# Transposing normalised rows on VectorE from a quadrant-wise load, one scratch each for Q and K, and an earlier load of the output weights

## The chip, the cores and the metric

The kernel runs on one NeuronCore of a Trainium2 chip. The metric is the time of one execution on the device, in microseconds (us). The engines are named as the profile names them: PE is TensorE (matrix products), PEld its weight loads, DVE is VectorE, ACT is ScalarE, POOL is GpSimd, and SP is the engine that issues nearly all DMAs.

## The reference

One row of 2048 tokens of width 640 goes through two branches in parallel, whose results are added to the input:

```python
x = A_x
xn = _layernorm(x, axis=-1)                    # (x - mean) / sqrt(var + 1e-5)
return x + _A_ref(xn, A_wqkv, A_wo) + _B_ref(xn, B_w_gate, B_w_up, B_w_down)
```

The first branch is attention with 32 heads of 20 features in a causal window of 256 tokens. The second is a gated MLP of inner width 1536:

```python
# A: q, k, v = heads of xn @ wqkv;  p = softmax(q k^T / sqrt(20), window 256);  (p v) @ wo
# B: (sigmoid(xn @ w_gate) * (xn @ w_up)) @ w_down
```

Inputs and output are bf16.

## The kernel before

The tokens are cut into four chunks of 512. For a chunk, `xnT[c]` holds the normalised rows with features on the partitions (five groups of 128 features) and tokens along the free dimension. All projections read it: Q and K (`proj_block`, tile `pqk`, L319), V (`project_v`, tile `pv`, L349), gate and up (`g_gu`, tiles `pg` and `pu`, L436 and L443). A product's result lies in one of four PSUM banks with the tag `d`, and the bank comes free when VectorE or ScalarE has read it.

How `xnT` is made differs by chunk. For chunk 0, rows are normalised as they arrive and turned by TensorE (`transpose_rows`, L299). For chunks 1 to 3 the generator `g_norms` does it in small steps: `load_x` brings the chunk with one DMA (token on the partition, L159), VectorE takes two `bn_stats` and one `bn_aggr` for each block of 128 rows (L272, L278), GpSimd makes the four reciprocal roots with an addition and a power (`rstd_blocks`, L286 and L287), VectorE normalises each block (`norm_block`, L292), and `turn_block` turns it with a DMA transpose on SP's queue (L303). The tile `xc` that `load_x` fills has one buffer, so the next chunk's load waits for the last norm of this one.

A block of Q or K is evicted into a tile `st` (six buffers; VectorE for Q, L323, ScalarE for K, L325) and stored in a DRAM scratch (`sq`, `sk`, L327), from which `spread` (L337) reads it back with heads on the partitions. There are two scratches for each of Q and K, used by chunks in turn. Rows 20 to 31 of each head's group of 32 are set to zero once by `clear` (L198): for the first pair of scratches at the start, for the second by `clear_next`, later.

The output weights are rearranged through DRAM: `turn_wo` (L232) writes them to the scratch `wo_i` with eight DMAs, `load_wo` (L237) reads them into SBUF with four. `load_wd` (L225) brings the down weights with five.

Attention goes by steps of scores. In a step TensorE fills `ps` (L512), ScalarE takes the exponential into `pT` (L517), GpSimd masks diagonal and old edges (L524), and in some steps VectorE masks a shared piece (L529). A pair of head groups is finished by `pv` (tile `acc`, L543), whose result VectorE transposes, scales and transposes again (L555 to L571).

The order is written out by hand. The class `Fill` holds a list of labelled generators (gate and up, Q and K, V, output of a chunk), each yielding the cost of what it has just recorded, and the loop over steps pulls as much filling between two steps as an allowance says. `mix(a, b, first, every)` interleaves a generator `b` (here `g_norms`) with the steps of `a`: from step `first` on, one step of `b` after each `every` steps of `a`. Each engine runs its own instructions in the recorded order, and so does SP's queue: a DMA that waits holds back all that is recorded behind it.

## Time and profile before

| | |
|---|---|
| runs | 310.28, 312.11, 312.65 us; median 312.11 |
| profiled execution, its own time | 312.31 us |
| its span (first to last instruction) | 310.5 us |
| TensorE busy | 302.4 us (97% of the span) |
| TensorE clock granted | 1.0 throughout |
| VectorE, ScalarE, GpSimd busy | 172.0, 198.4, 165.3 us |
| DMA | 35.67 MB, mean 115 GB/s |

The span is what the trace covers, and the time of the execution is 1.8 us longer. Busy time is a sum over the whole span. What limits a stage is seen in the idle time of TensorE there and in what ended it. In a line of groups the columns are: kernel line, engine, operation, output and inputs, shapes, count, then busy time, mean time of one in ns, and idle time of the engine before them with what ended it.

### The profile page before, as it was taken

The numbers are of one execution on the slowest core, as the hardware profiler recorded it, in microseconds if no ns is written. First come the engines' busy times: TensorE is split into PE (matmuls) and PEld (weight loads), VectorE is DVE, ScalarE is ACT, GpSimd is POOL, SyncE is SP. The second block draws the span as 40 slices with busy tenths as digits, with TensorE's granted clock in tenths as the row PEclk, the third lists the DMA queues.
The fourth block names the chain that finished last, engine by engine and source line by source line (L and its number), as shares of the span: only waits on it lengthen the run. The fifth ranks groups of instructions, "written<-read, shape, count | busy, mean of one in ns | idle before, by whom it ended". The sixth has DMA issues, their size and how long they took to land.

```text
span 310.5 us, 10034 instructions
## 1 busy us (share of the span) xinstructions
PE 302.4 (97%) x4343; PEld 168.1 (54%) x4343; DVE 172.0 (55%) x342; ACT 198.4 (64%) x196; POOL 165.3 (53%) x304
## 2 busy tenths in 40 slices
PE   6999999998999999999989999999999999999996
PEld 3654444544657654554556665454546665444774
DVE  5633684828697464496945346373643626372533
ACT  6923868668964648888654548978675647778000
POOL 3020668457885828566661836747383756657000
PEclk9999999999999999999999999999999999999999
DMA  7997984985705453440013512640000210000201
GB/s 206 365 327 237 330 155 150 344 260 165 231 0 89 108 158 121 155 160 2 3 23 88 87 56 89 211 155 1 4 0 4 67 40 23 2 2 2 87 23 63
DMA packets 40459, 35.67 MB, mean 115 GB/s; under 512 B 10560, under 2 KB 39872, under 8 KB 40384
## 3 DMA queue, kind: packets, MB, share of 16 engines
q1 hardware_dynamic: 39552, 34.27, 37.2%
q10 hardware_dynamic: 864, 0.77, 0.9%
q8 instruction: 34, 0.56, 0.8%
q14 instruction: 9, 0.07, 0.1%
HBM read 23.63 MB, written 10.26 MB: 109 GB/s over the span
## 4 chain that ended last, share of the span: by engine, by line
PE 90%; DVE 4%; DMA 2%; ACT 2%; issue 1%; SPq 0%; DVEq 0%; ACTq 0%
PE y L457 17%; PE pu L443 17%; PE pg L436 16%; PE pqk L319 12%; PE ps L512 8%; PE pv L349 7%; PE y L464 7%; PE acc L543 6%; DMA sq<-st 1%; ACT pT L517 1%; DVE on L567 1%; DMA xc<-in_A_x_dram 1%; DVE st L323 1%; DVE xn L292 1%; DVE h L447 0%
## 5 line engine op out<-in xcount | busy, mean ns | idle before, releaser
L524 POOL TENSOR_SCALAR_AFFINE_SELECT pT<-pT 64x512 bf16<-64x512 bf16 (+1 forms) x252 | 153.6, 609 | 103.6 <-ACT pT L517 91.8
L517 ACT ACTIVATE pT<-ps 128x2048 bf16<-128x2048 f32 x75 | 140.8, 1877 | 60.4 <-PE ps L512 57.5
L447 DVE SCALAR_TENSOR_TENSOR h<-th,pu 128x512 bf16<-128x512 f32 x48 | 32.8, 683 | 54.3 <-PE pu L443 41.7
L443 PE MATMUL pu<-xnT,wu 128*128 128x512 bf16 x240 | 59.8, 380 | 0.0
L436 PE MATMUL pg<-xnT,wg 128*128 128x512 bf16 x240 | 59.8, 380 | 0.0
L457 PE MATMUL y<-wd,h 128*128 128x320 bf16 (+2 forms) x396 | 56.8, 295 | 0.8 <-DVE h L447 0.8
L319 PE MATMUL pqk<-xnT,wqkv 128*128 128x512 bf16 x200 | 46.0, 381 | 0.0
L457 PEld LDWEIGHTS <-h 128*128 128x128 bf16 x396 | 36.6, 98 | 17.0 <-issue 2.2
L439 ACT ACTIVATE th<-pg 128x512 f32<-128x512 f32 x48 | 28.6, 596 | 15.3 <-PE pg L436 15.1
L436 PEld LDWEIGHTS <-wg 128*128 128x128 bf16 x240 | 22.3, 98 | 25.6 <-issue 2.0
L443 PEld LDWEIGHTS <-wu 128*128 128x128 bf16 x240 | 22.1, 98 | 25.4 <-issue 1.8
L319 PEld LDWEIGHTS <-wqkv 128*128 128x128 bf16 x200 | 22.6, 119 | 18.8 <-issue 1.4
L512 PE MATMUL ps<-qT,kT 20*64 20x320 bf16 (+4 forms) x1456 | 32.2, 259 | 0.3 <-issue 0.2
L512 PEld LDWEIGHTS <-kT 20*64 20x64 bf16 x1456 | 15.9, 103 | 24.8 <-issue 21.8
L555 DVE STREAM_TRANSPOSE t<-acc 128x512 f32<-128x512 f32 x32 | 21.1, 696 | 13.3 <-PE acc L543 13.3
L567 DVE TENSOR_TENSOR on<-t,rec 128x320 bf16<-128x320 f32 (+4 forms) x48 | 27.7, 576 | 1.1
L468 DVE SCALAR_TENSOR_TENSOR rows<-y,rows 128x320 bf16<-128x320 f32 x30 | 14.4, 488 | 23.8 <-PE y L464 23.5
L349 PE MATMUL pv<-wqkv,xnT 128*128 128x320 bf16 x160 | 25.9, 300 | 0.0
L464 PE MATMUL y<-wo,oc 128*128 128x320 bf16 (+2 forms) x165 | 24.2, 295 | 0.0
L543 PE MATMUL acc<-pT,v 64*32 64x320 bf16 (+4 forms) x1456 | 19.8, 252 | 1.4 <-DVE pT L529 1.4
L358 DVE CAST v<-pv 64x320 bf16<-64x320 f32 x29 | 14.1, 487 | 12.2 <-PE pv L349 11.9
L543 PEld LDWEIGHTS <-v 64*32 64x32 bf16 x1456 | 16.3, 91 | 7.4 <-issue 2.6
(48 smaller groups left out, 157.3 us busy)
## 6 DMA issues: line engine op xcount, KB each, us to landing
qT<-sq SPq DMA_DIRECT2D x16, 256.0 KB
kT<-sk SPq DMA_DIRECT2D x16, 256.0 KB
sq<-st SPq DMA_DIRECT2D x20, 128.0 KB
sk<-st SPq DMA_DIRECT2D x20, 128.0 KB
out_dram<-rows SPq DMA_DIRECT2D x15, 160.0 KB
wg<-in_B_w_gate_dram SPq DMA_DIRECT2D x4, 480.0 KB
wu<-in_B_w_up_dram SPq DMA_DIRECT2D x4, 480.0 KB
xc<-in_A_x_dram SPq DMA_DIRECT2D x3, 640.0 KB
```

The costliest lines, as they stand in the source:

```text
L319: nc.tensor.matmul(ps, lhsT=wt[:, m, :], rhs=xnT[c][:, d, :], start=(d == 0), stop=(d == DC - 1))
L349: nc.tensor.matmul(ps[:, 0:HALF], lhsT=xnT[c][:, d, s * P:(s + 1) * P], rhs=wqkv[:, d, 2 * D + hf * HALF:2 * D + (hf + 1) * HALF], start=( ...
L436: nc.tensor.matmul(pg, lhsT=part(wg, d, f), rhs=xnT[c][:, d, :], start=(d == 0), stop=(d == DC - 1))
L443: nc.tensor.matmul(pu, lhsT=part(wu, d, f), rhs=xnT[c][:, d, :], start=(d == 0), stop=(d == DC - 1))
L447: nc.vector.scalar_tensor_tensor(out=h, in0=th, scalar=1.0, in1=pu, op0=ADD, op1=MULT)
L457: nc.tensor.matmul(y[:, 0:cut[1] - cut[0]], lhsT=ht[c, f][:, s * P:(s + 1) * P], rhs=wd[:, f, cut[0]:cut[1]], start=(f == 0), stop=False)
L464: nc.tensor.matmul(y[:, 0:cut[1] - cut[0]], lhsT=oc[c, m][:, s * P:(s + 1) * P], rhs=wo[:, m, cut[0]:cut[1]], start=False, stop=(m == DC - 1))
L512: nc.tensor.matmul(ps[a * U:(a + 1) * U, i, col * U:(col + n) * U], lhsT=qk["k", kc, o // GH][32 * i:32 * i + DH, o % GH + a, kb * U:(kb + ...
L517: nc.scalar.activation(out=pt[:, :, 0:CW], in_=ps, func=EXP, scale=SCALE)
L524: nc.gpsimd.affine_select(out=view, in_=view, pattern=[[0, HG], [0, n], [sign, U]], compare_op=GE, fill=0.0, base=base, channel_multiplier ...
L543: nc.tensor.matmul(acc[32 * i:32 * i + 32, q * U:(q + n) * U], lhsT=vt[kb][a * U:(a + 1) * U, u, h * VW:h * VW + 32], rhs=pt[a * U:(a + 1) ...
L567: nc.vector.tensor_tensor(out=on[m][:, :, slot:slot + n], in0=t1[:, :, first:first + n], in1=rec.to_broadcast([P, 16, n]), op=MULT)
```

## The change

- `load_x` brings a chunk with four DMAs. The quadrant of partitions 32q to 32q + 31 gets features 160q to 160q + 159, and token 32j + t of the chunk lies on partition t of each quadrant, slot j.
- With features spread over the quadrants, VectorE's transpose of 32 x 32 blocks gives `xnT` directly. `turn_block` uses it in place of the DMA transpose.
- Feature 5p + b is now on partition p of group b, so all weights that multiply `xnT` are loaded in that order (`by_feature`), and chunk 0's transposes read rows with a stride of five.
- Statistics of a row are in four quadrants. `moments` takes them with eight `bn_stats` a chunk (two rows interleaved in each), two small operations turn them into mean and mean square, and `sum_quarters` adds the quadrants with one f32 product on TensorE against a matrix of quarters, made once by sixteen small GpSimd instructions. `rstd_rows` makes the roots of 16 columns with four GpSimd instructions.
- `norm_rows` normalises 128 x 160 elements at a time, sixteen for a chunk. It reads with a stride of five and writes runs of 32.
- Q and K have one scratch each. `clear_next` is gone.
- `turn_wo` is recorded right after `load_rest`. `load_wo` is recorded between the down weights and the Q and K of chunk 1, ahead of that chunk's Q stores; before, it was recorded inside `g_qk(1)` behind four of them.
- The steps of `g_norms` are spaced anew, and in `out1` the norms of chunk 3 go with every step of the output instead of every third.

The core of the diff:

```diff
 def load_x(c):
-        nc.sync.dma_start(out=t, in_=xr[:, c * SBC:(c + 1) * SBC, :])
+        for q in range(4):
+            nc.sync.dma_start(out=t[32 * q:32 * q + 32].rearrange("p s (j e) -> p (s j) e", e=QF),
+                              in_=x2[c * CW:(c + 1) * CW, q * QF:(q + 1) * QF].rearrange("(j t) e -> t j e", t=32))
...
+    def by_feature(w):
+        return w.rearrange("(p b) n -> p b n", b=DC)
...
-    scratch = {(w, k): tc.dram_tile([H * 32, CW], BF16, name=f"s{w}{k}")
-               for w in "qk" for k in range(2)}
+    scratch = {w: tc.dram_tile([H * 32, CW], BF16, name=f"s{w}") for w in "qk"}
...
+    def make_quarters():
+        for q in range(4):
+            rows = slice(32 * q, 32 * q + 32)
+            for k in range(4):
+                nc.gpsimd.tensor_scalar(out=quarters[rows, 32 * k:32 * k + 32], in0=ident[rows, rows],
+                                        scalar1=0.25, scalar2=None, op0=MULT)
...
+    def moments(c, u, stats):
+        nc.vector.bn_stats(out=stats[:, u, :],
+                           in_=xc[c].rearrange("p s (j e) -> p (s j) e", e=QF)[:, 2 * u:2 * u + 2, :]
+                           .rearrange("p j e -> p e j"))
+    def sum_quarters(stats):
+        ps = ps_d.tile([P, CW], FP32, name="pm", tag="d")
+        nc.tensor.matmul(ps[:, 0:2 * NJ], lhsT=quarters,
+                         rhs=stats.rearrange("p u (k z) -> p (u k) z", k=2)[:, :, 1:3], start=True, stop=True)
+        mom = lnp.tile([P, NJ, 2], FP32, name="mom", bufs=1)
+        nc.vector.tensor_copy(out=mom.rearrange("p j z -> p (j z)"), in_=ps[:, 0:2 * NJ])
+        return mom
+    def rstd_rows(mom):
+        r = lnp.tile([P, NJ], FP32, name="rstds", bufs=1)
+        nc.gpsimd.tensor_tensor(out=r, in0=mom[:, :, 0], in1=mom[:, :, 0], op=MULT)
+        nc.gpsimd.tensor_tensor(out=r, in0=mom[:, :, 1], in1=r, op=SUB)
+        nc.gpsimd.tensor_scalar(out=r, in0=r, scalar1=EPS, scalar2=None, op0=ADD)
+        nc.gpsimd.tensor_tensor(out=r, in0=r, in1=neghalf, op=POW)
+        return r
+    def norm_rows(c, s, j, mom, rstd):
+        if j == 0:
+            xns[c, s] = lnp.tile([P, D], BF16, name="xn")
+        k = s * SBC + j
+        nc.vector.tensor_scalar(out=xns[c, s].rearrange("p (b j f) -> p j b f", j=SBC, f=32)[:, j],
+                                in0=xc[c][:, s, j * QF:(j + 1) * QF].rearrange("p (f b) -> p b f", b=DC),
+                                scalar1=mom[:, k, 0:1], scalar2=rstd[:, k:k + 1], op0=SUB, op1=MULT)
...
 def turn_block(c, s):
-        nc.sync.dma_start(out=xnT[c][:, :, s * P:(s + 1) * P], in_=xns.pop((c, s)), transpose=True)
+        nc.vector.transpose(out=xnT[c][:, :, s * P:(s + 1) * P],
+                            in_=xns.pop((c, s)).rearrange("p (b t) -> p b t", b=DC))
...
 def g_norms(c, turn, behind=0):
-        mvs = lnp.tile([P, SBC, nc.vector.BN_AGGR_DIM], FP32, name="mvs", bufs=1)
-        for s in range(SBC):
-            ln_block(c, s, mvs[:, s, :])
-            if s < SBC - 1:
-                yield 0
-        for _ in range(behind):
+        stats = lnp.tile([P, NJ // 2, nc.vector.BN_STATS_DIM], FP32, name="moments", bufs=1)
+        for u in range(0, NJ // 2, 2):
+            moments(c, u, stats)
+            moments(c, u + 1, stats)
             yield 0
-        rstds = rstd_blocks(mvs)
+        mean, dev = (stats.rearrange("p u (k z) -> p u k z", k=2)[:, :, :, z] for z in (1, 2))
+        sq = lnp.tile([P, NJ // 2, 2], FP32, name="sq", bufs=1)
+        nc.vector.tensor_tensor(out=sq, in0=mean, in1=mean, op=MULT)
+        nc.vector.scalar_tensor_tensor(out=dev, in0=dev, scalar=1.0 / QF, in1=sq, op0=MULT, op1=ADD)
+        for _ in range(2 + behind):
+            yield 0
+        mom = sum_quarters(stats)
+        rstd = rstd_rows(mom)
         for _ in range(4):
             yield 0
         for s in range(SBC):
-            norm_block(c, s, mvs[:, s, :], rstds[:, s:s + 1])
-            yield 0
+            for j in range(SBC):
+                norm_rows(c, s, j, mom, rstd)
+                if j == 1:
+                    yield 0
             if turn:
                 turn_block(c, s)
+            yield 0
...
 def g_qk(c):
-                if c == 1 and w == "q" and m == 3:
-                    load_wo()
...
     load_rest()
+    turn_wo()
...
-    norms3 = g_norms(3, False)
+    norms3 = g_norms(3, False, 2)
...
     fill.add("x2", later(load_x, 2), 0)
-    fill.add("wo_i", later(turn_wo), 0)
     fill.add("wd", later(load_wd), 0)
-    fill.add("pads", later(clear_next), 0)
+    fill.add("wo", later(load_wo), 0)
     fill.add("qk1", g_qk(1), 50 * MM)
...
-    fill.add("out1", mix(g_out(1, g_gu(2, 0, 1)), itertools.chain(norms3, g_turns(3)), 1, 3), OUT + GU)
+    fill.add("out1", mix(g_out(1, g_gu(2, 0, 1)), itertools.chain(norms3, g_turns(3)), 1, 1), OUT + GU)
```

## The prediction

> **What bounds the kernel now.** I read the page first (sections 1 and 4), then busy time in stretches of 3 us, then the waits, then groups by line with shapes kept apart, then the timeline of VectorE and GpSimd where the change works.
>
> ```profile
> PE 302.4 (97%) x4343; PEld 168.1 (54%) x4343; DVE 172.0 (55%) x342; ACT 198.4 (64%) x196; POOL 165.3 (53%) x304
> ...
> PE 90%; DVE 4%; DMA 2%; ACT 2%; issue 1%; SPq 0%; DVEq 0%; ACTq 0%
> ```
>
> TensorE is busy 302.4 of 310.5 us, and the chain that ended last is 90% TensorE. The idle 8.1 us is all that can be won. The stretches tell where it lies (first number after the stretch's length: TensorE busy):
>
> ```profile
> 69.00:72.00 3.00, 1.56 (x84) 0.91 (x68) 1.38 (x3) 2.27 (x4) 1.75 (x4) 1.00 0.54 158
> 156.00:159.00 3.00, 2.16 (x17) 1.37 (x15) 2.34 (x5) 1.10 (x1) 2.33 (x5) 1.00 0.30 60
> 306.00:309.00 3.00, 1.42 (x23) 1.25 (x20) 1.06 (x3) 0.00 (x0) 0.00 (x0) 1.00 0.36 109
> ```
>
> 2.4 us lie in the first 9 us and 3.1 us after 306, which the change leaves alone; 1.44 us at 69 and 0.84 us at 156 are the stalls it touches, with about 0.3 us in crumbs. So the most it can win is some 2.6 us, 0.8%. The waits name both stalls:
>
> ```profile
> ACT st L325 <- DMA sq<-st: 2.0, 1, 2.0
> ...
> PE acc L543 <- DVE pT L529: 1.4, 1, 1.4
> ...
> PE y L457 <- DVE h L447: 0.8, 1, 0.8
> ```
>
> At 69: ScalarE could not evict a K block because the buffer still belonged to a Q store that had not landed; the exp behind it was late, then VectorE's mask, then TensorE. At 156: the last h of chunk 1 stood on VectorE behind two norms of chunk 3 (1.59 us on the chain).
>
> **The change, part by part.** The prices:
>
> ```profile
> L571 DVE STREAM_TRANSPOSE oc<-on 128x512 bf16<-128x512 bf16 x20 | 14.2, 711 | 0.7
> ...
> L292 DVE TENSOR_SCALAR xn<-xc,mvs,rstds 128x640 bf16<-128x640 bf16 x12 | 7.4, 640 | 0.9 <-POOL rstds L287 0.9
> ...
> L287 POOL TENSOR_TENSOR rstds<-rstds,neghalf 128x4 f32<-128x4 f32 x3 | 3.2, 1061 | 0.3
> ...
> L292 DVE TENSOR_SCALAR xn<-xc,mv,rstd 128x640 bf16<-128x640 bf16 x2 | 0.9, 446 | 0.1
> ...
> L286 POOL TENSOR_SCALAR rstds<-mvs 128x4 f32<-128x4 f32 x3 | 0.7, 227 | 3.1 <-DVE mvs L278 2.9
> ```
>
> *Transposes.* Twelve DMA transposes (1.2 us of SP's queue each) go; they never held TensorE. VectorE gets four per chunk of 128x640. The bf16 128x512 one takes 711 ns, and the next instruction starts 0.64 us after it; 128 columns more at the 1.04 ns a column that its neighbours show (f32 sums: 490 ns for 320 columns, 291 for 128) make 0.77 us. So 3.1 us a chunk.
>
> *Norms.* Four of 128x640 become sixteen of 128x160 with a stride of five elements in. The trace has no strided one. Above: a norm of VectorE alone that does not speed up costs 157 ns + 160 x 1.04 = 0.32 us, 0.28 from start to start; contended it could be 0.5, since the 128x640 norms range from 405 to 930 ns while GpSimd works. Below: a quarter of 446 ns, with overlap, 0.14. I take n = 0.28, the row of single columns being nearest. 16n = 4.5 us a chunk against about 2.4 now.
>
> *Statistics.* Still eight bn_stats of 320 columns (472 ns); four aggregates (209 ns) give way to two small sums and a copy: equal.
>
> *GpSimd.* Two instructions on 4 columns become four on 16: three plain ones (227 ns each with little per column: 0.8 us) and the power. The power on 4 columns takes 1.06 us. If its cost over a plain one (0.83 us) is per instruction, 16 columns take 1.06; if per column, 0.23 + 4 x 0.83 = 3.6. A plain instruction on as many columns takes 0.23, so the extra is more likely per column; I take p = 2.5, nearer to that end.
>
> *A: chunk 1.* Here hidden work comes out on the path. In the built order the reciprocal roots now stand behind the masks of the third step of scores. Those ran here:
>
> ```profile
> 39.64 4.89 POOL L524 TENSOR_SCALAR_AFFINE_SELECT pT<-pT 64x512 bf16<-64x512 bf16 x8 [0.17 <-ACT pT L517]
> ...
> 42.57 1.11 DVE L292 TENSOR_SCALAR xn<-xc,mvs,rstds 128x640 bf16<-128x640 bf16 x2
> 44.02 0.69 DVE L447 SCALAR_TENSOR_TENSOR h<-th,pu 128x512 bf16<-128x512 f32 x1 [0.34 <-issue]
> 44.62 1.31 DVE L555 STREAM_TRANSPOSE t<-acc 128x512 f32<-128x512 f32 x2
> ```
>
> Half of these eight masks (39.64 to 42.1) are ahead of the roots, so the roots are ready at 42.1 + 0.8 + p = 45.4. Behind them on GpSimd are the fourth step's masks, for which TensorE's acc at 43.4 waits (it already shows a 0.4 us weight-load wait on them), and on VectorE everything behind the first norm: h, and the transposes that free acc's banks. From that norm to the last transpose VectorE has 16n + 4 x 0.77 + four h at 0.61 + 1.24 (acc) + two reciprocals 0.5 + three scalings 1.15 + one oc 0.64 = 9.0 + 16n us, back to back. TensorE wants the whole xnT at 54.96 (first pqk of chunk 1). Late by 42.9 + p + 9.0 + 16n - 55.0 = p + 16n - 3.1 = +3.9 us. The acc stall lies inside this. Ends: p = 1.06, n = 0.14 gives +0.2; p = 3.6, n = 0.5 gives +8.5.
>
> *B: chunk 2.* VectorE is full from 83.8 to 94 and does its norms behind the second block's rows and the scaling of a head pair; without norms that work ends at 101.7. Then come 16n, 3.1 and 0.9 (rows): 105.7 + 16n against pqk at 109.34, so 16n - 3.6 = +0.9 us (0 to +4.4).
>
> *C: chunk 3.* The norms now stand behind the last h of chunk 1: the 0.84 us stall goes. Twelve norms then lie among the rows of the first two blocks and delay a y bank by about 0.4: net -0.4 (-0.8 to +0.6). The transposes end near 176, five us ahead of pqk.
>
> *D: SP's queue at the Q stores.* The weight turn (8 issues, 5.0 us) moves to 36 to 42, where transposes were. But x for chunk 2 (now four issues) waits for the last norm of chunk 1, 9 us later than now relative to pqk, and wd (five issues), wo (four) and the ten Q and K stores of chunk 1 stand behind it. Counted from the first pqk: x at -0.8, wd 1.0 to 3.4, wo to 6.0, first Q store at 6.2 (now 5.06). Ahead of its data lie x, wd and wo, 3.4 MB, at the 330 GB/s of that stretch 10.4 us; the two clears, 0.79 MB, are gone. It lands about 0.4 us earlier than now, and the stall shrinks to 1.0: -0.4 (-1.4 to +0.6). One scratch adds no wait: the spreads that read it were done some 20 us before.
>
> *E: the head.* x for chunk 1 goes from 512 packets of 1280 B to 2048 of 320 B, ahead of Q and K stores. Packets under 512 B (one transpose alone, 156 to 159) and 1280 B ones (17 to 20) moved at:
>
> ```profile
> GB/s 0 0 0 0 0 0 0 0 0 0 0 0 0 0 0 0 0 0 0 58 174 225 225 218 212 225 205 225 201 151 55 10 0 0 218 0 0 0 0 0
> ...
> GB/s 358 348 358 399 348 379 399 348 358 393 382 355 577 369 331 355 389 341 335 345 280 246 246 161 123 140 123 106 140 96 215 113 147 119 150 218 253 287 335 317
> ```
>
> 655 KB at 215 instead of 370 GB/s is 1.3 us more. The queues are 45 to 54% idle at 25 to 27, which takes most of it; the first scores at 30.8 wait on that chain (0.4 us): +0.3 (0 to 1.3). The Trainium skill, "DMA: Bandwidth & Descriptors", Specifications, puts line rate at 512 B and up, with a read-modify-write below. By that rule the load would cost twice its time, 3.5 instead of 1.8 us; the trace's 215 against 370 agrees in kind, and the sum would be about 0.4 higher.
>
> *F: small.* Chunk 0's transposes load weights with a stride of five: such loads take 119 ns (wqkv) against 98 (xn): 20 x 21 ns, half of it covered, +0.2 (0 to 0.4). Three f32 matmuls of 32 columns: two inside stalls already counted, one +0.3 (0.1 to 0.9). Sixteen GpSimd instructions for the quarter matrix lie in its idle 18 to 33 us.
>
> Sum: 3.9 + 0.9 - 0.4 - 0.4 + 0.3 + 0.2 + 0.3 = +4.8 us on the profiled 312.31: **317.1**. The median of the runs is 312.11, so the same by either.
>
> **Rivals.** *VectorE keeps up* (not slower): a norm costs 0.14 and the power 1.06. Then A = 0.2, B = 0, C = -0.8, D = -0.4, E to F +0.6: 311.9. It decides once p + 16n falls below about 4. For it: 0.45 us for 640 columns shows a norm runs faster than a column per 1.04 ns. Against it: that row is unstrided. In the Trainium skill, "VectorE: DVE Perf Modes", What auto-detection actually checks, packing two 16-bit elements needs step 1, while using both ports needs only matching outer dimensions. By it the norm would keep half its speed-up, n about 0.2, which puts the sum at 314.9, in between.
>
> *GpSimd and VectorE hold each other up*: n = 0.5, p = 3.6. A = 8.5, B = 4.4: 325.2. For it: 446 ns in the head, where GpSimd rests, against 640 mean and 930 at most later. The Trainium skill, "SBUF — State Buffer", Who interferes with whom, says two-port VectorE operations and GpSimd shut each other out; those rows agree. Against it: sixteen short ones need not each meet a mask.
>
> *Small packets at half rate again*: E +1.3, and D turns to +0.6 as x for chunk 2 lands late: 319.4.
>
> **How the numbers follow.** Forecast 0.50, VectorE keeps up 0.30, mutual blocking 0.12, packets 0.08. About 1%, 3.1 us, is what a measurement of this kernel can tell from no change. Faster by that (under 309.0) is beyond all that can be won as counted: 0.05 for what I do not see. Same: nearly all of the first rival and a small part of the forecast, 0.33. Slower: 0.62. The range 310.0 to 323.0 takes in the first and third rival and cuts the second; the forecast's own is 314.5 to 320.5.
>
> **What would show it.** A: idle TensorE, or pqk waiting on VectorE's transpose, at 55 to 60, and the power near 2.5 us. B: the same near 110. C: no wait of y on h at 156. D: the eviction's wait on the Q store at 1 to 2 us. n and p can be read directly. The forecast is wrong if chunk 1's first pqk starts before 56.

## The result, and the profile after

The changed kernel takes **329.92 us** (median of 4 runs, 329.39 to 330.76) against 312.06 us for the kernel before on the same chip (310.28 to 312.65): ratio 1.0585, interval 1.0537 to 1.0633. It is 17.9 us slower, where +4.8 was forecast and +10.9 was the end of the range. The profiled execution took 329.81 us, span 328.1.

Busy time, the clock row and the shares of the chain, from the page of the changed kernel:

```profile
PE 307.8 (94%) x4349; PEld 170.0 (52%) x4349; DVE 195.7 (60%) x387; ACT 198.3 (60%) x196; POOL 176.3 (54%) x326
...
PEclk9999999699999997999999999999999999999999
...
PE 70%; DVE 10%; DMA 7%; POOL 5%; issue 3%; SPq 2%; ACT 2%; DVEq 0%; ACTq 0%; POOLq 0%
```

TensorE's share of the chain fell from 90 to 70%. Two things grew: its idle time, from 8.1 to 20.3 us, and its busy time, from 302.4 to 307.8 us though its work is the same but for three small matmuls. The clock row says why most of the second: in slices 8 and 16 the granted clock drops. (Of the busy time, the groups pqk and acc gained 4.0 us and the three new products took 1.0.) Stretches of 3 us around both places (busy time of PE, PEld, DVE, ACT, POOL, then granted clock, DMA share, GB/s):

```profile
60.00:63.00 3.00, 0.00 (x0) 0.00 (x0) 2.97 (x7) 1.07 (x1) 0.92 (x2) 0.54 0.00 0
63.00:66.00 3.00, 2.86 (x37) 1.11 (x45) 1.48 (x4) 0.00 (x0) 0.00 (x0) 0.50 1.05 203
...
120.00:123.00 3.00, 0.12 (x1) 0.00 (x0) 2.96 (x7) 0.00 (x0) 2.10 (x4) 1.00 0.15 55
123.00:126.00 3.00, 1.20 (x4) 0.53 (x4) 2.49 (x7) 0.00 (x0) 0.00 (x0) 0.85 0.00 0
126.00:129.00 3.00, 3.00 (x25) 0.88 (x22) 0.69 (x1) 1.48 (x1) 0.00 (x0) 0.59 0.83 200
```

At 60 and at 120 TensorE stands still while VectorE is full (2.97 and 2.96 of 3). These are the two starts of pqk that steps A and B of the prediction are about. When TensorE resumes, its clock is 0.50 for some 4 us, so the first matmuls take up to 631 ns instead of 379. The waits:

```profile
PE pqk L360 <- DVE xnT L343: 7.9, 2, 4.7
DVE xn L325 <- POOL rstds L318: 7.8, 2, 4.6
...
ACT st L366 <- DMA sq<-st: 3.5, 2, 2.5
...
PE acc L590 <- POOL pT L571: 2.2, 2, 2.0
```

The third line is the stall on the Q stores, which was to shrink. Groups by line, and the spread of the norm (minimum, median, maximum in ns):

```profile
L325 DVE TENSOR_SCALAR xn<-xc,mom,rstds 128x160 bf16<-128x160 bf16 x48 | 22.1, 511 | 7.8 <-POOL rstds L318 7.8
...
L318 POOL TENSOR_TENSOR rstds<-rstds,neghalf 128x16 f32<-128x16 f32 x3 | 8.8, 2939 | 0.2
```
```profile
L325 DVE TENSOR_SCALAR xn<-xc,mom,rstds x48: 341/448/817, 46.5 to 187.9; 128x160 bf16<-128x160 bf16 x48
```

The power takes 2.94 us (2.5 was taken). The norm runs from 341 to 817 ns. Chunk 2's sixteen on VectorE's timeline, in fours, with a GpSimd line beside the third four:

```profile
113.23 2.51 DVE L325 TENSOR_SCALAR xn<-xc,mom,rstds 128x160 bf16<-128x160 bf16 x4
...
119.66 2.20 DVE L325 TENSOR_SCALAR xn<-xc,mom,rstds 128x160 bf16<-128x160 bf16 x4
...
122.67 1.20 DVE L325 TENSOR_SCALAR xn<-xc,mom,rstds 128x160 bf16<-128x160 bf16 x4
```
```profile
119.85 2.44 POOL L571 TENSOR_SCALAR_AFFINE_SELECT pT<-pT 64x512 bf16<-64x512 bf16 x4 [0.42 <-ACT pT L564]
```

Four norms take 1.20 us (0.30 each, near the 0.28 that was taken) when GpSimd rests, and 2.2 to 2.5 beside masks; the four left out took 1.54, partly beside masks.

Landmarks of the profiled executions (first and last pqk of chunk 1, first of chunks 2 and 3, span, in us) show where the 17.6 us of span went. The other rows belong to the experiments below.

| kernel | pqk 1 first | pqk 1 last | pqk 2 first | pqk 3 first | span |
|---|---|---|---|---|---|
| before | 54.8 | 68.3 | 109.2 | 181.3 | 310.5 |
| changed | 63.1 | 78.5 | 124.8 | 198.3 | 328.1 |
| e4 dummies | 63.5 | 76.9 | 128.6 | 200.6 | 329.0 |
| e10 four norms | 59.6 | 73.1 | 115.4 | 186.6 | 315.7 |
| e13 and roots | 57.2 | 70.7 | 115.9 | 188.9 | 317.8 |
| e16 and weights | 56.4 | 69.9 | 109.4 | 182.3 | 311.6 |
| e17 dummies, weights | 63.5 | 76.9 | 121.2 | 193.2 | 321.6 |

Before against changed: +8.3 to the first pqk; +1.9 in chunk 1's pqk itself (half clock: 15.4 instead of 13.5 us); +5.4 to chunk 2's pqk, of which 4.7 is the wait for xnT; +1.4 to chunk 3's (half clock again, 1.6); +0.6 behind.

### The profile page after: what moved, and what is told of

It is laid out like the page before. It is cut to its first block, busy times and chain, and to the rows that moved or that the text cites. A ratio compares the mean times of both kernels' runs of the same rounds, so it can differ in the third digit from the quotient of the medians.

```text
span 328.1 us, 10102 instructions
## 1 busy us (share of the span) xinstructions
PE 307.8 (94%) x4349; PEld 170.0 (52%) x4349; DVE 195.7 (60%) x387; ACT 198.3 (60%) x196; POOL 176.3 (54%) x326
## 4 chain that ended last, share of the span: by engine, by line
PE 70%; DVE 10%; DMA 7%; POOL 5%; issue 3%; SPq 2%; ACT 2%; DVEq 0%; ACTq 0%; POOLq 0%
PE y L504 13%; PE pg L483 12%; PE pu L490 11%; PE pqk L360 11%; PE pv L390 7%; PE ps L559 6%; PE y L511 6%; DVE xn L325 5%; PE acc L590 5%; POOL pT L571 3%; DMA wo<-wo_i 2%; POOL rstds L318 2%; ACT pT L564 2%; DMA wqkv<-in_A_wqkv_dram 2%; DVE xnT L343 1%
## 5 line engine op out<-in xcount | busy, mean ns | idle before, releaser
L360 PE MATMUL pqk<-xnT,wqkv 128*128 128x512 bf16 x200 | 48.4, 395 | 7.9 <-DVE xnT L343 7.9
L486 ACT ACTIVATE th<-pg 128x512 f32<-128x512 f32 x48 | 28.6, 596 | 17.6 <-PE pg L483 14.5
L614 DVE TENSOR_TENSOR on<-t,rec 128x320 bf16<-128x320 f32 (+4 forms) x48 | 29.1, 606 | 1.1
L325 DVE TENSOR_SCALAR xn<-xc,mom,rstds 128x160 bf16<-128x160 bf16 x48 | 22.1, 511 | 7.8 <-POOL rstds L318 7.8
L590 PE MATMUL acc<-pT,v 64*32 64x320 bf16 (+4 forms) x1456 | 21.4, 258 | 4.3 <-POOL pT L571 2.2
L590 PEld LDWEIGHTS <-v 64*32 64x32 bf16 x1456 | 17.0, 94 | 11.5 <-issue 6.8
```

The lines of the kernel that those rows point to most:

```text
L325: nc.vector.tensor_scalar(out=xns[c, s].rearrange("p (b j f) -> p j b f", j=SBC, f=32)[:, j], in0=xc[c][:, s, j * QF:(j + 1) * QF].rearran ...
L360: nc.tensor.matmul(ps, lhsT=wt[:, m, :], rhs=xnT[c][:, d, :], start=(d == 0), stop=(d == DC - 1))
L590: nc.tensor.matmul(acc[32 * i:32 * i + 32, q * U:(q + n) * U], lhsT=vt[kb][a * U:(a + 1) * U, u, h * VW:h * VW + 32], rhs=pt[a * U:(a + 1) ...
```

## Experiments

The theory after the first look: VectorE is late ahead of pqk of chunks 1 and 2, since roots stand behind masks and norms are slowed by them; each gap costs half clock on top. Rivals: the strided norm is slow by itself; the order of SP's queue; small packets; the transposes on VectorE.

**e1, the other half of the change by itself**

```diff
 (kernel before)
-    scratch = {(w, k): tc.dram_tile(...) for w in "qk" for k in range(2)}
+    scratch = {w: tc.dram_tile([H * 32, CW], BF16, name=f"s{w}") for w in "qk"}
...
     load_rest()
+    turn_wo()
...
-    fill.add("pads", later(clear_next), 0)
+    fill.add("wo", later(load_wo), 0)
```

> The kernel before with only the second half of the change: one scratch each for Q and K without the second pair of clears, the turn of the output weights at the head, their load ahead of the Q stores of chunk 1. Loads of x, norms and DMA transposes as before. My theory (the loss lies on VectorE and GpSimd ahead of the first pqk of chunks 1 and 2): 311.4 us, between -1.4 and 0 against before, with the eviction's wait on the Q store at 69 us shorter than its 2.0. Rival (the order of SP's queue makes the loss: stores and spreads behind the weights, or a scratch that two chunks share): 315 or more, with pqk or ps of chunk 1 or 2 waiting on spreads or stores.

Measured 312.66 us, ratio 1.0012 (0.9995 to 1.003). Scratch and weights together cost nothing that can be told, and gain nothing. The eviction's wait, 2.0 us before, is still there:

```profile
ACT st L320 <- DMA sq<-st: 1.8, 1, 1.8
```

The gain that step D expects of this pair doesn't show; e15 takes the pair apart.

**e2, no masks**

```diff
-        for diag, u, n in step["masks"]:
+        for diag, u, n in ():
```

> The changed kernel without the masks on GpSimd (this part of the computation is left out), so GpSimd has next to nothing but the roots, the reciprocal roots start at once and no norm meets a mask. Theory (the roots stand behind masks, and norms are slowed by GpSimd from 0.29 to about 0.48 us from start to start): the median of the 128x160 norm falls from 448 to about 340 ns, the first pqk of chunk 1 starts 5 to 6 us earlier, at 57 to 58, that of chunk 2 without a wait over 1 us, and the time is 316 to 319 us. Rival (a norm with a stride of five in its source costs 0.45 us whoever runs beside it): the median stays above 430 ns, only the roots gain, and the time is about 325.

Measured 319.0 us (1.0223, 1.0168 to 1.0277): 10.9 less than the changed kernel. The norm without masks beside it:

```profile
L325 DVE TENSOR_SCALAR xn<-xc,mom,rstds x48: 343/374/727, 44.2 to 176.9; 128x160 bf16<-128x160 bf16 x48
```

Its median falls from 448 to 374 ns and its sum from 22.1 to 15.5 us. That is the theory's side, though the first pqk starts at 58.9 and still waits 2.3 us for xnT, where 57 to 58 was expected. But masks are gone here altogether, so this can't part the roots' place from the norms' slowing.

**e3, roots on VectorE**

```diff
...
-        nc.gpsimd.tensor_tensor(out=r, in0=r, in1=neghalf, op=POW)
...
+        nc.vector.tensor_scalar(out=r, in0=v, scalar1=-0.5 * Y0 ** 3, scalar2=1.5 * Y0, op0=MULT, op1=ADD)
+        nc.vector.tensor_tensor(out=t, in0=r, in1=r, op=MULT)
+        nc.vector.scalar_tensor_tensor(out=t, in0=t, scalar=-0.5, in1=v, op0=MULT, op1=MULT)
+        nc.vector.scalar_tensor_tensor(out=r, in0=t, scalar=1.5, in1=r, op0=ADD, op1=MULT)
```

> The changed kernel with the reciprocal roots on VectorE: six small instructions of 16 columns (two steps of Newton's from a constant) in place of four on GpSimd. Theory: the roots no longer stand behind masks nor take 2.94 us, so the first pqk of chunk 1 comes about 3 us earlier, at 60, that of chunk 2 by 2 us, and TensorE's acc no longer waits 2.0 us on GpSimd; about 325 us (323 to 327). Rival (the norms and transposes of VectorE alone set the start, and the roots are hidden in its other work): 329 to 331.

Measured 329.21 us (327.61 to 330.07): 0.7 less, which can't be told from nothing, and a miss. The first pqk came 2.4 us earlier (60.7), as expected, and chunk 2's 2.3 (122.5), so chunk 2 added no gain of its own; its last pqk came only 1.7 earlier and chunk 3's first 0.7. What was gained in chunk 1 was mostly given back later: the half clock behind chunk 2's gap lasts 6.8 us here (3.4 in the changed kernel), and y waits 1.6 us on h (0.2 there).

**e4, matmuls that keep the clock up**

```diff
     def g_qk(c):
+        if c in (1, 2):
+            ps = ps_d.tile([P, CW], FP32, name="pwarm", tag="d")
+            for k in range(14):
+                nc.tensor.matmul(ps, lhsT=ones[:, 0:P], rhs=ones, start=(k == 0), stop=(k == 13))
```

> The changed kernel with 14 more matmuls of 512 columns, whose result nobody reads, ahead of the first pqk of chunks 1 and 2, that is inside the two gaps in which TensorE waits for the transposes. Theory (a gap of about 4 us halves TensorE's granted clock for the next 3.8 us of work, which costs 1.9 and 1.7 us): the granted clock stays at 0.98 or more behind both gaps, the gaps themselves stay, and the time falls by 3 to 3.6 us to about 326.5. Rival (what follows the gap waits for something else anyway, or the matmuls come too late and add their own 3 us a time): 329.5 to 333.

Measured 330.31 us, no gain. The clock did stay up: chunk 1's pqk took 13.4 us again. But TensorE then ran into the next thing sooner, in stretches of e4 and its wait:

```profile
78.00:81.00 3.00, 0.43 (x16) 0.21 (x24) 0.00 (x0) 1.24 (x3) 0.00 (x0) 0.95 0.43 148
81.00:84.00 3.00, 1.91 (x84) 1.14 (x87) 0.68 (x1) 2.58 (x3) 1.22 (x3) 0.50 0.65 209
```
```profile
ACT st L367 <- DMA sq<-st: 7.3, 2, 6.0
```

The eviction now waits 6.0 us on a Q store, and the clock halves behind that gap instead. The store's landing is set by SP's queue: x for chunk 2 can't be issued before the last norm of chunk 1 is done (62.2 us in the changed kernel), and wd and wo follow it, ahead of the stores. Late norms thus delay TensorE twice: through xnT and through the queue.

**e5, wd and wo ahead of x for chunk 2**

```diff
     load_rest()
     turn_wo()
+    load_wd()
+    load_wo()
...
-    fill.add("wd", later(load_wd), 0)
-    fill.add("wo", later(load_wo), 0)
```

> The changed kernel with the loads of wd and wo right behind the turn of the output weights, so ahead of x for chunk 2 instead of behind it; nothing else moved. The dummy matmuls showed that the Q stores of chunk 1 land at a time that SP's queue sets: x for chunk 2 can be issued only when the last norm of chunk 1 is done (62.2 us), and 2.8 MB of wd and wo follow it ahead of the stores. Theory: with them out of the way the eviction's wait on the stores (3.5 us) falls under 0.5 and TensorE's idle 1.7 us at 78 to 82 goes; what follows moves along, so 1.5 to 2.5 us less, about 327.8. Rival (the gap ahead of chunk 2's pqk is set by VectorE and takes up what is won): 329 to 331.

Measured 329.9 us (1.0568, 1.054 to 1.0595): alone it gains nothing that can be told either. The execution that was profiled took 771 us and isn't read here, so where the gain went isn't shown; the other three, at 329.2 to 330.4 us, have a mean clock of 0.978 to 0.984, so the half clock stayed.

**e6, chunk 2's norms in chunk 1's K and V blocks**

```diff
-    norms2 = g_norms(2, True, 1)
+    norms2 = g_norms(2, True)
...
-    fill.add("qk1", g_qk(1), 50 * MM)
-    fill.add("v1", mix(g_v(1), g_gu(1, 0, 2), 1, 2), 40 * 136 + 2 * GU)
-    fill.add("out0", mix(g_out(0, g_gu(1, 2, 3)), norms2, 1, 1), OUT + GU)
+    fill.add("qk1", mix(g_qk(1), norms2, 4, 1, False), 50 * MM)
+    fill.add("v1", mix(mix(g_v(1), g_gu(1, 0, 2), 1, 2), norms2, 0), 40 * 136 + 2 * GU)
+    fill.add("out0", g_out(0, g_gu(1, 2, 3)), OUT + GU)
```

> The changed kernel with the statistics, norms and transposes of chunk 2 mixed into the K blocks and the V blocks of chunk 1, where VectorE rested some 5 us, instead of the output rows of chunk 0. Theory (chunk 2's pqk waits because VectorE is full from 99 to 125 us with norms, transposes and the heads' scaling): the wait of 4.7 us and the half clock behind it (1.6 us) go, about 324.3 us (323 to 326). Rival (VectorE's work is only moved, and the second half of chunk 1 waits for it instead): 328 or more, with waits of PE on VectorE's h, pT or acc between 80 and 125.

Measured 333.1 us, 3.2 more. The rival was right: the work is only moved. TensorE now idles at 93 to 96 (1.45 of 3 us busy), and chunk 2's pqk starts at 128.5.

**e7, everything earlier**: e3, e5 and e6 together, without the pauses between statistics, roots and norms, and with chunk 3's norms four steps later.

```diff
-        for _ in range(2 + behind):
+        for _ in range(behind):
...
-        for _ in range(4):
-            yield 0
...
-    norms3 = g_norms(3, False, 2)
+    norms3 = g_norms(3, False, 6)
```

> The changed kernel with the roots on VectorE, none of the pauses between statistics, roots and norms of chunk 1, the norms of chunk 2 in chunk 1's K and V blocks, and wd and wo ahead of x for chunk 2. All VectorE transposes, strided norms and quarter-wise loads stay. Theory (the loss is a matter of when VectorE's work is due, not of its amount): pqk of chunks 1 and 2 wait less than 1.5 us each, the clock stays at full, and the time is 313 to 317. Rival (the amount of VectorE's and GpSimd's work, with norms slowed by masks, sets it): 320 or more.

Measured 326.0 us (1.0424, 1.0385 to 1.0463). The profiled execution took 328.8 us, more than the others, so the sizes of its waits are rough. In it pqk no longer waits for xnT, but other waits came in its place: TensorE 3.6 us on a copy of V behind the moved norms, and 3.3 us on the moments ahead of the small matmul that sums them, which holds up all of TensorE. That is the rival's side: amount, not only placement.

**e8, the kernel before in the changed order**

```diff
 (e1)
     turn_wo()
+    load_wd()
+    load_wo()
...
-    norms3 = g_norms(3, False)
+    norms3 = g_norms(3, False, 2)
...
-    fill.add("out1", mix(g_out(1, g_gu(2, 0, 1)), itertools.chain(norms3, g_turns(3)), 1, 3), OUT + GU)
+    fill.add("out1", mix(g_out(1, g_gu(2, 0, 1)), itertools.chain(norms3, g_turns(3)), 1, 2), OUT + GU)
```

> The kernel before with one scratch each and the output weights turned early, wd and wo issued right behind that turn, so the Q stores of chunk 1 have only x ahead of them, and chunk 3's norms two steps later, behind the last h of chunk 1; loads, norms and DMA transposes as before. Theory: the eviction's wait on the Q store (2.0 us, 1.4 of TensorE) and the wait of y on h (0.84 us) go, so 309.8 us, -1.5 to -2.5 against before. Rival (the stores are late because of their own queue's packets and not of what lies ahead): 311.5 to 312.5.

Measured 320.4 us (1.0268, 1.0238 to 1.0297), a clear miss: 8 us slower than before. Its wait:

```profile
PE pqk L314 <- DMA xnT<-xn: 8.2, 1, 8.2
```

Chunk 1's DMA transposes now stand behind wd and wo on SP's queue and are issued from 54.1 us on. So with DMA transposes the weights must not be ahead; with VectorE's they may.

**e9, prices by themselves**, in a bench that computes nothing of the reference: eight norms of each form and eight transposes, GpSimd idle and then beside six masks; powers; bursts of matmuls behind gaps; loads.

> Not the block but a bench of single prices (it computes nothing of the reference): the strided 128x160 norm, the same without stride, the 128x640 norm and the 128x640 transpose, eight of each with GpSimd idle and eight beside six masks; the power on 4, 8, 16 and 32 columns; bursts of 40 matmuls of 512 columns behind gaps of 1 to 9 us; one chunk of x in packets of 1280 and of 320 bytes, twice each. Theory: strided norm 0.28 to 0.30 us from start to start with GpSimd idle and 0.45 to 0.6 beside masks, the transpose the same with and without; power 0.43 + 0.157 us a column (1.06, 1.7, 2.94, 5.5); the granted clock stays full behind gaps under 3 us and is 0.5 for some 3.8 us of work behind gaps over 4. Rivals: strided norm 0.45 or more with GpSimd idle; power flat from 16 to 32; a lower clock behind any gap, or behind none, in which case the half clock of the changed kernel has another cause.

VectorE's timeline, eight instructions a line, first with GpSimd idle and then beside masks, and GpSimd's powers:

```profile
5.16 2.39 DVE L52 TENSOR_SCALAR strided<-x,mom 128x160 bf16<-128x160 bf16 x8 [4.17 <-DMA x<-in_A_x_dram]
...
8.08 4.80 DVE L52 TENSOR_SCALAR strided<-x,mom 128x160 bf16<-128x160 bf16 x8
...
13.47 1.94 DVE L57 TENSOR_SCALAR plain<-x,mom 128x160 bf16<-128x160 bf16 x8
...
15.94 3.07 DVE L57 TENSOR_SCALAR plain<-x,mom 128x160 bf16<-128x160 bf16 x8
...
20.74 3.82 DVE L61 TENSOR_SCALAR whole<-x,mom 128x640 bf16<-128x640 bf16 x8
...
25.22 5.17 DVE L61 TENSOR_SCALAR whole<-x,mom 128x640 bf16<-128x640 bf16 x8
...
31.00 7.00 DVE L65 STREAM_TRANSPOSE turn<-x 128x640 bf16<-128x640 bf16 x8
...
38.53 6.99 DVE L65 STREAM_TRANSPOSE turn<-x 128x640 bf16<-128x640 bf16 x8
```
```profile
46.23 1.01 POOL L102 TENSOR_TENSOR r<-base,half 128x4 f32<-128x4 f32 x1
...
49.13 2.90 POOL L102 TENSOR_TENSOR r<-base,half 128x16 f32<-128x16 f32 x1
...
52.17 5.43 POOL L102 TENSOR_TENSOR r<-base,half 128x32 f32<-128x32 f32 x1
```

The strided norm costs 0.30 us from start to start with GpSimd idle (2.39 / 8) and 0.60 beside masks (4.80 / 8). The 128x640 norm goes from 0.48 to 0.65, the transpose not at all (0.87 both). Without the stride (`plain`) the short norm takes 0.24 alone and 0.38 beside masks. So masks add 0.14 us to the short norm, 0.17 to the long one and 0.30 to the short one with the stride: little for four norms, as much as the work itself for sixteen strided ones. Beside masks, a block of 128 rows costs 0.65 us as one norm, 1.5 as four short ones, and 2.4 as four short ones with the stride. Splitting and stride thus have about equal parts in the price; with GpSimd idle (0.48, 0.97, 1.2) the stride is the smaller part. No run has sixteen norms without the stride in the kernel itself. The power is 0.37 + 0.158 us a column.

Bursts of 40 matmuls on TensorE, with the gap ahead of each in brackets, and the clock in two stretches:

```profile
68.06 8.79 PE L114 MATMUL burst<-chain,w 128*128 128x512 bf16 x39 [2.03 <-ACT chain L117]
80.18 10.28 PE L114 MATMUL burst<-chain,w 128*128 128x512 bf16 x39 [3.33 <-ACT chain L117]
95.09 11.13 PE L114 MATMUL burst<-chain,w 128*128 128x512 bf16 x39 [4.62 <-ACT chain L117]
```
```profile
82.00:83.00 1.00, 1.00 (x4) 0.29 (x2) 0.00 (x0) 0.00 (x0) 0.00 (x0) 0.50 0.00 0
...
84.00:85.00 1.00, 1.00 (x6) 0.49 (x5) 0.00 (x0) 0.00 (x0) 0.00 (x0) 1.00 0.00 0
```

Here a gap of 2.0 us costs nothing, one of 3.3 us costs 1.5 us of half clock, one of 4.6 us 2.3. The half clock lasts 3.4 us behind the gap of 3.3, 6.8 behind that of 4.6 and 10.2 behind the longest, of 8.5: each a multiple of 3.4.

A chunk of x took 5.6 us from issue to use in packets of 320 B (first line) and 4.2 in packets of 1280:

```profile
52.00 0.15 DVE L127 CAST go<-y 128x1 f32<-128x1 bf16 x1 [5.62 <-DMA y<-in_A_x_dram]
56.40 0.15 DVE L123 CAST go<-y 128x1 f32<-128x1 bf16 x1 [4.24 <-DMA y<-in_A_x_dram]
```

**e10, four 128x640 norms in place of sixteen**

```diff
         if j == 0:
...
+            nc.vector.tensor_scalar(out=xns[c, s], in0=xc[c][:, s, :],
+                                    scalar1=mom[:, k, 0:1], scalar2=rstd[:, k:k + 1], op0=SUB, op1=MULT)
```

> The changed kernel with one 128x640 norm in place of each four strided 128x160 ones, at their place (the mean and root of the first of the four rows are taken for all, so that the normalisation is not computed rightly); roots, transposes, loads and masks stay. Theory (the 16 norms are 7.2 us of a chunk where 4 would be 2.6, on the engine that sets the start of pqk): the first pqk of chunk 1 comes 4 to 5 us earlier, that of chunk 2 waits under 1 us, no half clock: 316 to 320 us. Rival (the norms fill time that the transposes, the roots or the loads would leave empty): over 325.

Measured 320.7 us (1.0271, 1.0206 to 1.0336): **9.2 us** back, 0.7 short of what was expected. No pqk waits for xnT any more. This is the largest single piece of the loss. It takes away the splitting and the stride together.

The half clock is not gone from it. TensorE's acc waits 2.01 us for masks that stand behind the roots, in the changed kernel (first line of each fence) as here (second line), and only here does the clock drop:

```profile
46.91 0.32 PE L590 MATMUL acc<-pT,v 64*32 64x320 bf16 x4 [2.01 <-POOL pT L571]
46.84 0.32 PE L589 MATMUL acc<-pT,v 64*32 64x320 bf16 x4 [2.01 <-POOL pT L570]
```
```profile
48.00:51.00 3.00, 3.00 (x44) 1.39 (x37) 2.93 (x8) 2.50 (x3) 1.16 (x3) 1.00 0.10 43
48.00:51.00 3.00, 2.78 (x7) 1.10 (x9) 2.88 (x6) 2.47 (x2) 1.17 (x3) 0.51 0.05 20
```

It is half from 48.0 to 51.4, and the first pqk is still 4.8 us later than in the kernel before. In e6, whose program is the changed kernel's up to there, the same gap halves the clock too. What decides it is not shown; the four executions of e10 took 317.4 to 322.0 us at mean clocks of 0.995 to 0.983.

**e11 and e12, DMA transposes**, with sixteen norms and with four

```diff
-        nc.vector.transpose(out=xnT[c][:, :, s * P:(s + 1) * P],
-                            in_=xns.pop((c, s)).rearrange("p (b t) -> p b t", b=DC))
+        nc.sync.dma_start(out=xnT[c][:, :, s * P:(s + 1) * P], in_=xns.pop((c, s)), transpose=True)
```

> The changed kernel with DMA transposes in place of the twelve on VectorE, at their place (their order of rows isn't that of this load, so xnT is not computed rightly); strided norms, roots, loads stay. Theory (VectorE is relieved of 3.1 us a chunk, but each transpose then has to land): pqk of chunks 1 and 2 1 to 2 us earlier each, about 326 (323 to 328). Rival (the transposes on VectorE are the loss itself): 317 or less. Other rival (they stand in SP's queue where the weights now are, and land late): 330 or more.

> The changed kernel with both of these: four 128x640 norms a chunk and DMA transposes (neither computed rightly, as above); the quarter-wise loads, the statistics and the roots on 16 columns stay. Theory (what is left against before is the roots' 2 us behind the masks and the small packets): 313 to 316. Rival (small packets or the order of SP's queue carry the loss): 320 or more.

Measured 332.1 (1.0636, 1.0572 to 1.07) and 323.3 us (1.0362, 1.0318 to 1.0407), each 2 to 3 more than the same with VectorE's (329.9 and 320.7), though the intervals overlap. In e11 pqk waits 9.1 us on the landing of the transposes:

```profile
PE pqk L359 <- DMA xnT<-xn: 9.1, 2, 5.0
```

Transposes on VectorE are thus not what made the kernel slow; in this order of SP's queue they are no dearer than DMA transposes, and probably cheaper.

**e13, four norms and the roots on VectorE** (e10 and e3)

> The run with four 128x640 norms a chunk (not computed rightly) and, on top of it, the roots on VectorE. With sixteen norms the roots' place was worth 0.7 us. Theory (they were covered by the norms; with these out of the way the roots' wait behind masks and the 2 us that TensorE's acc waits for GpSimd at 45 to 48 come out): 316.5 us (315 to 318). Rival (the rest is the head, the small packets and the Q stores, and the roots are covered still): 319.5 to 321.

Measured 320.0 us (1.0251, 1.021 to 1.0292): the rival, and no difference from e10 that can be told. The first pqk came 2.4 us earlier than in e10 (57.2), and the Q stores took it up. TensorE from 72 to 81, here and then, to 75, in e16:

```profile
72.00:75.00 3.00, 1.16 (x56) 0.69 (x57) 0.00 (x0) 2.80 (x4) 0.00 (x0) 1.00 0.39 111
75.00:78.00 3.00, 2.11 (x45) 1.10 (x45) 1.99 (x3) 2.04 (x4) 2.62 (x6) 0.70 0.75 252
78.00:81.00 3.00, 2.95 (x35) 1.48 (x33) 2.60 (x7) 1.91 (x4) 2.13 (x4) 0.73 0.38 115
```
```profile
72.00:75.00 3.00, 3.00 (x41) 1.74 (x40) 2.92 (x7) 2.94 (x4) 2.34 (x5) 1.00 0.20 65
```

**e14, norms on ScalarE**

```diff
-        nc.vector.tensor_scalar(..., scalar1=mom[:, k, 0:1], scalar2=rstd[:, k:k + 1], op0=SUB, op1=MULT)
+        nc.scalar.activation(..., func=IDENTITY, scale=rstd[:, k:k + 1], bias=shift[:, k:k + 1])
...
+        nc.vector.scalar_tensor_tensor(out=shift, in0=mom[:, :, 0], scalar=-1.0, in1=rstd, op0=MULT, op1=MULT)
```

> The changed kernel with the roots on VectorE and all sixteen strided norms of each chunk on ScalarE (an activation with scale and bias, and one small product for the bias); everything is computed. Theory (the norms cost because they stand on the engine that is full and block against GpSimd; ScalarE rests a third of the span): VectorE has only the transposes more than before, pqk of chunks 1 and 2 wait under 1.5 us, 314 to 318 us. Rival (sixteen instructions a chunk cost as much wherever they stand, and the exps and K evictions of ScalarE now wait behind them): 322 or more.

Measured 328.7 us (1.0535, 1.05 to 1.057), a miss: no different from e3 (329.2), which has the roots on VectorE too. On ScalarE no mask disturbs the norm, but it is longer from the start:

```profile
L330 ACT ACTIVATE xn<-xc,shift,rstds x48: 545/556/581, 44.5 to 187.8; 128x160 bf16<-128x160 bf16 x48
```

VectorE's transposes wait 12.3 us on it. In this order sixteen short strided norms a chunk cost as much on either engine.

**e15, the kernel before with one scratch and later norms of chunk 3**

```diff
 (kernel before)
+    scratch = {w: tc.dram_tile([H * 32, CW], BF16, name=f"s{w}") for w in "qk"}
...
-    norms3 = g_norms(3, False)
+    norms3 = g_norms(3, False, 2)
...
-    fill.add("pads", later(clear_next), 0)
...
-    fill.add("out1", mix(g_out(1, g_gu(2, 0, 1)), itertools.chain(norms3, g_turns(3)), 1, 3), OUT + GU)
+    fill.add("out1", mix(g_out(1, g_gu(2, 0, 1)), itertools.chain(norms3, g_turns(3)), 1, 2), OUT + GU)
```

> The kernel before with one scratch each for Q and K (no second clears), and chunk 3's norms two steps later, behind the last h of chunk 1; the output weights stay where they were. Theory (0.79 MB of clears less ahead of the Q stores, and y no longer waits 0.84 us on h): 310.6 us, 1 to 2 less than before. Rival (the Q stores' landing is set by wd and wo, and the norms then hold up a y instead): 311.7 to 312.5.

Measured 311.35 us (0.9982, 0.9966 to 0.9999): 0.6 us less than before, the fastest of all, and hardly more than can be told from nothing. Neither the wait on the Q store nor that of y on h shows any longer; 1.1 us of a wait of scores on kT took part of their place. Against e1 this takes step D apart: with the clears gone the Q store is in time (here), and with wo moved ahead of it as well it is late again (e1).

**e16, four norms, the roots on VectorE, the weights early** (e13 and e5)

> The run with four 128x640 norms a chunk (not computed rightly) and the roots on VectorE, and wd and wo issued ahead of x for chunk 2 as well. Theory (with the norms gone the late stores are what binds): TensorE's 3.7 us idle at 69 to 78 shrink under 1, and the time falls by 2.5 to 3.5 us to about 317. Rival (VectorE's work ahead of chunk 2's pqk takes it up, as it did with sixteen norms): 319.5 to 320.5.

Measured 313.5 us (1.0054, 1.003 to 1.0077): 6.5 us less than e13, by an edit that alone (e5) gave nothing, and twice what was expected. TensorE's gap at 69 to 78 is gone (second fence of e13), 3.7 us. So is the half clock behind it, which the expectation left out: in e13 it lasts from 76.2 to 79.6, about 1.7 us of work lost, and in e16 the clock is 1.00 throughout. 16.4 of the 17.9 us are won back, with all transposes on VectorE, in a kernel that takes one row's mean and root for four rows.

**e17, dummy matmuls and early weights** (e4 and e5)

> The changed kernel with the 14 dummy matmuls ahead of pqk of chunks 1 and 2 and with wd and wo ahead of x for chunk 2: sixteen norms and roots as changed. Theory (in chunk 1 the half clock and the Q stores each cover the other, and VectorE sets the start of chunk 2's pqk behind both): the eviction's wait on the stores is under 1 us, TensorE waits for chunk 2's xnT longer than the changed kernel's 4.7 us less the dummies' 3, and only the half clock behind that gap is won: 328 to 329. Rival (both losses add up): 325 to 326. Other rival (neither matters): 330.

Measured 323.4 us (1.0378, 1.0352 to 1.0404): 6.5 us less, where each alone gave nothing (330.3 and 329.9). A line of VectorE ahead of chunk 2's norms, in the changed kernel and in e17:

```profile
107.71 1.31 DVE L602 STREAM_TRANSPOSE t<-acc 128x512 f32<-128x512 f32 x2 [1.46 <-PE acc L590]
```
```profile
104.11 1.31 DVE L607 STREAM_TRANSPOSE t<-acc 128x512 f32<-128x512 f32 x2 [1.46 <-PE acc L595]
```

Everything behind chunk 1 moves up by 3.60 us, the half clock (1.9) and TensorE's idle at the Q stores (1.7) together, with the same waits. The theory that VectorE holds chunk 2's start in place falls: VectorE follows TensorE there. Chunk 2's half clock gives another 1.5. The other 1.4 us lie behind chunk 3's first pqk: the changed kernel has a wait of scores there that e17 doesn't have.

```profile
PE ps L559 <- ACT th L486: 1.4, 1, 1.4
```

**e18, small packets in the kernel before**

```diff
-        nc.sync.dma_start(out=t, in_=xr[:, c * SBC:(c + 1) * SBC, :])
+        for q in range(4):
+            nc.sync.dma_start(out=t[:, :, q * (D // 4):(q + 1) * (D // 4)],
+                              in_=xr[:, c * SBC:(c + 1) * SBC, q * (D // 4):(q + 1) * (D // 4)])
```

> The kernel before with each chunk's x loaded by four DMAs of 160 columns each, so in 2048 packets of 320 bytes instead of 512 of 1280, to the same places. In the bench of single prices such a load takes 1.4 us longer. Theory (the predicted +0.3 in the head, nothing elsewhere): 312.3, between 0 and +1.0 against before. Rival (small packets hold up Q and K stores and spreads, a part of the change's loss): 313.5 or more.

Measured 313.6 us (1.0054, 1.0023 to 1.0085): +0.7 to +2.7, so more than the +0.3 of the sum, and in size the rival. The place is the theory's: in the trace (an execution of 312.9 us) the first scores wait 0.7 us for kT, the first pqk starts at 55.6 (54.8 before), and nothing is added behind it. It is as much as e16 still lacks; that it is the same 1.4 us was not shown.

## Why the prediction was wrong

The direction was right, the place was right (A and B named the two gaps), and the time was 12.8 us short.

*A and B, the norm: mis-sized.* The formulas held. With the measured p = 2.94 and chunk 1's sixteen norms at 7.2 us (0.45 each), p + 16n - 3.1 gives +7.0; the first pqk was 8.2 late, with 0.6 of the rest from the head. With 7.45 us of norms in chunk 2, 16n - 3.6 gives +3.9; the wait was 4.7. The step that failed is n = 0.28: right for a norm alone (0.30 in the bench, so at the single-column bound and not at the 0.2 that a kept half of the speed-up would give), but the norms do not run alone. The measured n is 0.45 in chunk 1 and 0.47 in chunk 2. That is the mechanism of the rival "GpSimd and VectorE hold each other up" (n = 0.5, 325.2 us). Its argument against itself, that sixteen short norms need not each meet a mask, was right and not enough: of chunk 1's eight pairs three took 0.63 to 0.66 us, undisturbed, and five 0.95 to 1.32. The stride counts for more beside masks than alone (e9). The Trainium skill, "SBUF — State Buffer", Who interferes with whom, says that a two-port VectorE operation and GpSimd take the shared ports for a whole instruction and that the other blocks. The bench agrees in kind: 0.30 to 0.60 us for the norm, nothing for the transpose.

With the measured p and n the prediction's own sum comes to +10.9, so 323.2 us. The measured 329.9 is 6.7 above that, and 3.5 of it is the next step.

*The half clock: missing.* Behind gaps of 3.2 and 4.7 us TensorE lost 1.9 and 1.6 us at half clock; no step had it, and the trace of before, with a clock of 1.00 throughout, gave no price for it. The Trainium skill, "TensorE: Matmul & The Clock Gate", Part 1, says that the clock halves after an idle window of about 3.4 us and comes back after as long of work. The bench is near that for the fall, 3.0 to 4.3 us after the last matmul; coming back took 3.0 to 5.7 us after the next. The kernels show that the length of one gap does not settle it. In the changed kernel the clock falls at 60.2, only 0.3 us into the gap of 3.2, with a gap of 1.7 and 1.2 us of work ahead of it; in e13 it falls behind two gaps of 1.7; and a gap of 2.0 halves it in e10 and e6 but not in the changed kernel.

*D, the Q stores: wrong sign.* Forecast -0.4; TensorE lost 1.7 us instead of 1.4, and in e1 clears removed and wo moved ahead gain nothing between them; with the clears removed alone (e15) the wait does go. D counted x for chunk 2 behind the last norm, rightly, but treated the stall as a term of a sum. It is a second chain from the same late norm, beside the one through xnT: either can be shortened without effect until the other is (e4 and e5 against e17, e5 and e13 against e16).

*C* came out nearly as forecast: the stall of y on h fell from 0.84 to 0.2 us (in e16, with the roots elsewhere, it is back at 1.6). Behind chunk 3's first pqk a wait of scores of 1.4 us is new, which C didn't have. *E* was low: +1.4 alone (e18) against +0.3, in the place that it named. The doubled load time that E also weighs did not show: the bench has 5.6 against 4.2 us, 1.33 times. *F* can't be told apart from the +0.6 at the head; the three f32 products took 1.0 us of TensorE.

*The transposes*, costed at 3.1 us a chunk, cost VectorE that much, but on the whole nothing: without the sixteen norms and with the weights out of the way (e16) they are within 1.3 us of the kernel before, small packets included.

In order: four norms -9.2, the roots on VectorE -0.7 (within the noise), the weights early -6.5. The last 1.3 is open in part. By the landmarks e16 is 1.6 us late at chunk 1's first pqk, where small packets are the candidate, level with the kernel before (0.2) at chunk 2's, since the stall on the Q stores is gone, and 0.9 late at chunk 3's, as y waits 1.6 us on h (0.8 before).

## What to carry to other kernels

Cost a short VectorE instruction by its time beside a busy GpSimd, not by its time alone: in the bench the delay came with each instruction, and splitting one norm in four turned 0.65 into 1.5 us, with a stride of five in its source into 2.4. Ask of each late instruction what else it releases, here a load and the whole queue behind it; when two chains leave the same late point, an edit to one shows nothing and the pair shows everything, so test pairs before calling a cause harmless. And when a change opens gaps in TensorE, look at the granted clock behind them: here gaps of 2 to 5 us brought 3.4 us of half clock, or a multiple of it, in some cases and none in others, so an estimate needs a range.

## What the runs showed of the hardware that was not expected

One and the same TensorE gap of 2.0 us left the clock at 1.00 in the changed kernel and halved it for 3.4 us in e10 and e6; the half clock lasted 3.4, 6.8 or 10.2 us wherever it was read. Masks on GpSimd added 0.14 us to an unstrided 128x160 norm, 0.30 to one with a stride of five, and nothing to a 128x640 transpose. The power on GpSimd is paid by the column, 0.158 us each (4 columns 1.01 us, 32 columns 5.43). ScalarE's norm of 128x160 takes 545 to 581 ns in e14, with and without masks beside it, against 341 to 817 on VectorE in the changed kernel.
